# Linear attention and a GELU MLP in one kernel: batch 0 by single head pairs, first weights in two loads, h of chunk 0 over all eight banks, and the casts at its end shared anew

## The chip, the cores and the metric

The kernel runs on one core of one Trainium2 chip. The metric is the device time of one execution in microseconds (us). Engines are named as in the profile: PE is TensorE (PEld its weight loads), DVE is VectorE, ACT is ScalarE, POOL is GpSimd, SP is SyncE, which here only issues DMAs. Each engine works through a queue of its own in program order; semaphores make one wait for another.

## The reference

```
q, k, v: (8 batches, 8 heads, 576 positions, 64)          float32
q_s = softmax over the 64 of q;   k_s = softmax over the 576 positions of k
kv  = einsum('bhsd,bhse->bhde', k_s, v)
a   = einsum('bhsd,bhde->bhse', q_s, kv)
x   = a.transpose(0, 2, 1, 3).reshape(4608, 512)
h   = x @ w_in                 (512 x 2048)
g   = 0.5 * h * (1 + erf(h / sqrt(2)))
out = g @ w_out                (2048 x 512)               float32
```

## The kernel before

The tokens are worked through in nine chunks of 512: chunk b holds the first 512 positions of batch b, and the last chunk the remaining 64 of all eight batches. Matmuls are in bf16. Heads go in pairs: head pair hp (0 to 3) fills 128 partitions. The order of the work on every engine is written out by hand (`manual_schedule`); nothing is moved by a planner, so the order of the calls in the file is the order in each queue.

For batch 0 the steps are these.

- `load_main`, `load_pair`, `load_wi` and `load_wo` issue the loads on SP's queue: q, k and v of batch 0, then w_in in five pieces (`wi[0]` to `wi[4]`, 256, 256, 512, 512 and 512 columns), then w_out and the inputs of batch 1. A load of one piece of v is 0.29 MB. Each load waits in SP's queue for a semaphore that the eighth load before it sets.
- `exp_q` and `exp_k` (ACT) take the exponentials. `norm_q` sums q (DVE) and scales it (`q_scale`, line 295): heads 0 to 3 on POOL, heads 4 to 7 on DVE. `tp_mm` transposes q on PE, half of the head pairs at a time, and `tp_evac` copies it out of PSUM into `qT`.
- `cast_v` turns one head pair of v into bf16 (`v_aug`): pairs 0 and 1 on ACT (line 200), pairs 2 and 3 on POOL (line 202). `kv_mm` (line 237) makes kv for two head pairs, `kv_norm` scales it into `kvc` on DVE (lines 248 and 250). `x_mm` (line 380) makes x for two head pairs, `x_evac` copies a pair to `xT` on ACT (line 425) or DVE (line 423).
- `cast_wi_dm` and `cast_wi` turn w_in into bf16 (lines 1181 and 1169 on POOL, 1170 and 1173 on DVE), rows dm 0 to 3 of 128 each.

Then chunk 0 is done plainly (later chunks use sums that save matmuls). `h_phase` makes h for 16 tiles t of 128 columns, four matmuls each (dm 0 to 3, line 432). A group of tiles goes through dm in common, so each dm is asked for by all tiles of the group before the next one. Each tile has a PSUM bank; `h_gelu` (ACT, line 438) empties it into `g`. Functions given for a tile run after its gelu. Groups were 0 and 1 together, 2, 3, then 4 to 7, 8 to 11, and 12 to 15 one by one; banks came from 0, 1, 2 in turn, with others named for tiles 3, 6 and 8 to 11. Then `y_part(t, js)` (line 764) adds tile t of g @ w_out for the token groups js. It needs w_out in bf16: `cast_wo` (line 1207 on DVE, 1209 on ACT).

Between the y matmuls batch 1 is prepared: its exponentials, `norm_q`, `cast_v`, `tp_quarters` (PE, line 343) with `tp_quarters_evac` (DVE 353, ACT 355), kv, `kv_norm` and x. `mix_wo` (line 1226) forms sums of w_out that later chunks need. `y_out` copies y to SBUF (DVE 772, ACT 774) and stores it. `h_first` then begins h of chunk 1 (line 716).

`cast_v` is short, and its engine is the last argument:

```python
def cast_v(b, hp, eng=nc.vector):
    o = v_aug[b % 2][:, hp, :, 0:D]
    i = st[b]["vf"][:, hp, :].rearrange("p (n d) -> p n d", n=NS)
    if eng is nc.scalar:
        eng.copy(out=o, in_=i)
    else:
        eng.tensor_copy(out=o, in_=i)
```

Of the kernel before, what the change touches and what calls it, by code (L numbers as in the profile page):

```python
# [8 lines left out]
FP32 = mybir.dt.float32  # L9
# [7 lines left out]
def kernel(  # L17
# [43 lines left out]
    def bank(i, name="ps", shape=(128, 512)):  # L61
        return psum.tile(list(shape), FP32, tag=f"k{i}", name=name)
# [32 lines left out]
    def table(func):  # L95
        nc.scalar.activation(out=scr[:, 1:2], in_=scr[:, 0:1], func=func)  # L96
# [99 lines left out]
# [7 lines that stand above are left out]
# [23 lines left out]
    def kv_mm(b, half):  # L226


        if "kv" not in st[b]:
            kv_tiles(b)  # L230
        for n in range(NS):
            for i in range(2):
                for hh in range(2):
                    hp = 2 * half + i
                    pr = slice(hh * 64, hh * 64 + 64)
                    c = slice((hh ^ i) * 64, (hh ^ i) * 64 + 64)
                    nc.tensor.matmul(  # L237
                        st[b]["kv"][hp][c, 0:D + 1], ek[b % 2][pr, hp, n, :],
                        v_aug[b % 2][pr, hp, n, 0:D + 1], start=(n == 0), stop=(n == NS - 1),
                    )  # L240

    def kv_norm(b, half=None):

        if half is not None:
            hps = (2 * half, 2 * half + 1)
            rec = small.tile([128, 2], FP32, tag="reck")
            for i, hp in enumerate(hps):
                nc.vector.reciprocal(rec[:, i:i + 1], st[b]["kv"][hp][:, D:D + 1])
            for i, hp in enumerate(hps):
                nc.vector.tensor_tensor(  # L250
                    out=kvc[b][:, hp, :], in0=st[b]["kv"][hp][:, 0:D],
                    in1=rec[:, i:i + 1].to_broadcast([128, D]), op=ALU.mult,
                )
            return
        for i, ps in enumerate(st[b]["kvall"]):
            rec = small.tile([128, 2], FP32, tag="reck")
            nc.vector.reciprocal(rec, ps[:, :, D])
            nc.vector.tensor_tensor(
                out=kvc[b][:, 2 * i:2 * i + 2], in0=ps[:, :, 0:D],
                in1=rec.unsqueeze(2).to_broadcast([128, 2, D]), op=ALU.mult,  # L260
            )
# [67 lines left out]
    def tp_evac(b, half, eng="v"):  # L329
        o = st[b]["qT"][:, :, 2 * half:2 * half + 2, :]  # L330
        if eng == "v":
            nc.vector.tensor_copy(out=o, in_=st[b][f"tp{half}"])
        else:
            nc.scalar.copy(out=o, in_=st[b][f"tp{half}"])
# [30 lines left out]
    def x_tile(b, hp, pool, tag):  # L365
        if "xT" not in st[b]:
            st[b]["xT"] = attn_sb.tile([128, HP, M], BF16, tag="xT", name="xT", bufs=1)
        st[b][f"x{hp}"] = pool.tile([128, M], FP32, tag=tag, name="ps")

    def x_mm(b, half):  # L370

        for bb in range(B if b == B else 1):
            for r in range(2):
                for i in range(2):
                    hp = 2 * half + i
                    pr = slice(r * 64, r * 64 + 64)
                    c = slice((r ^ i) * 64, (r ^ i) * 64 + 64)
                    ps = st[b][f"x{hp}"]
                    if b < B:
                        nc.tensor.matmul(  # L380
                            ps[c, :], kvc_of(b, hp)[pr], st[b]["qT"][pr, :, hp, :],
                            start=True, stop=True,
                        )
                    else:
                        nc.tensor.matmul(
                            ps[c, bb * R:(bb + 1) * R], kvc_of(bb, hp)[pr],
                            st[b]["qT"][pr, bb // 2, hp, bb % 2 * R:(bb % 2 + 1) * R],
                            start=(bb == 0), stop=True, skip_group_check=True,
                        )
# [30 lines left out]
    def x_evac(b, hp, eng="v"):  # L420
        ps = st[b][f"x{hp}"]
        if eng == "v":
            nc.vector.tensor_copy(out=st[b]["xT"][:, hp, :], in_=ps)
        else:
            nc.scalar.copy(out=st[b]["xT"][:, hp, :], in_=ps)  # L425
# [4 lines left out]
    def h_mm(c, ps, t, dms):  # L430
        for dm in dms:
            nc.tensor.matmul(  # L432
                ps, wi_bf[:, dm, t * 128:(t + 1) * 128], st[c]["xT"][:, dm, :],
                start=(dm == 0), stop=(dm == NDM - 1),
            )
# [305 lines left out]

        inner(mm, seed, p5_copy, e_sum, r_sum, gelu)

    def h_phase(c, ins, groups={}, banks={}, t1=0):


        if t1 == 0:
            h_begin(c)
        while t1 < NDF:
            t0, t1 = t1, t1 + groups.get(t1, 1)  # L750
            ts = range(t0, t1)
            pss = []
            for t in ts:
                pss.append(banks[t]() if t in banks else psum_h.tile([128, M], FP32, tag="h", name="ps"))
            for dm in range(NDM):
                for ps, t in zip(pss, ts):
                    h_mm(c, ps, t, (dm,))
            for ps, t in zip(pss, ts):
                h_gelu(c, ps, t)
                for f in ins.get(t, []):  # L760
                    f()
# [7 lines left out]
    def y_out(c, ps, j, eng="v"):  # L769
        y_sb = yb4[:, j - j % 2:j - j % 2 + 2]  # L770
        if eng == "v":
            nc.vector.tensor_copy(out=y_sb[:, j % 2], in_=ps)
        else:
            nc.scalar.copy(out=y_sb[:, j % 2], in_=ps)
        if j % 2:
            y_store(c, j // 2, y_sb)
# [368 lines left out]
        store(1, 1, 0, both)  # L1145

    wi_cols = [256, 256, 512, 512, 512]
    wi_parts = [1, 1, 4, 2, 2]
    wi_off = [0, 256, 512, 1024, 1536]

    def load_wi(i):
# [23 lines left out]
    def cast_wi_dm(i, w, dm, eng):  # L1175

        n = wi_cols[i]
        r = n // 128
        o = wi_bf[:, dm, wi_off[i]:wi_off[i] + n].rearrange("p (c m) -> p c m", c=r)
        w = w[:, dm, 0:n].rearrange("p (m c) -> p c m", c=r)  # L1180
        eng.tensor_copy(out=o, in_=w)
# [22 lines left out]
    def cast_wo(i, w, c0=0, n=4, eng="v"):  # L1204
        o, w = wo_bf[:, 4 * i + c0:4 * i + c0 + n, :], w[:, c0:c0 + n]
        if eng == "v":
            nc.vector.tensor_copy(out=o, in_=w)
        else:
            nc.scalar.copy(out=o, in_=w)
# [55 lines left out]
    norm_q(0, 0, 2)  # L1265
    norm_q(0, 1, 2, nc.vector)
    tp_mm(0, 0)
    cast_v(0, 0, nc.scalar)
    cast_v(0, 1, nc.scalar)
    tp_evac(0, 0)  # L1270
    cast_v(0, 2, nc.gpsimd)
    cast_v(0, 3, nc.gpsimd)
    x_tile(0, 0, psum_y, "y")
    x_tile(0, 1, psum_y, "y")
    kv_mm(0, 0)
    kv_norm(0, 0)
    tp_mm(0, 1)
    tp_evac(0, 1, "s")
    x_tile(0, 2, psum_a, "a")
    kv_mm(0, 1)  # L1280
    kv_norm(0, 1)
    for dm in range(NDM):
        cast_wi_dm(0, wi[0], dm, nc.gpsimd)
    x_tile(0, 3, psum_h, "h")
    x_mm(0, 0)
    x_evac(0, 0, "s")
    x_evac(0, 1)
    x_mm(0, 1)
    x_evac(0, 2, "s")
    x_evac(0, 3)  # L1290
    cast_wi(1, wi[1], "pv")
    table(AF.Gelu)

    def ybank():
        return psum_y.tile([128, M], FP32, tag="y", name="ps")

    sums0 = quad_weights(0)
    h_phase(0, {
        0: [lambda: cast_wi(2, wi[2], "v")],
        2: [lambda: cast_wi(3, wi[3], "v")],  # L1300
        6: [lambda: cast_wi(4, wi[4], "v")],
        9: sums0[0:2] + [lambda: cast_wo(0, wo[0])],
        15: [lambda: cast_wo(1, wo[1], eng="s")],
    }, groups={0: 2, 4: 4, 8: 4}, banks={
        3: ybank, 6: ybank, 8: ybank,
        9: lambda: psum_a.tile([128, M], FP32, tag="a", name="ps"),
        10: lambda: bank(6), 11: lambda: bank(7),
    })


    exp_q(1, parts=2)
# [15 lines left out]
    norm_q(1, 0, 2)  # L1327
    norm_q(1, 1, 2, nc.vector)
    mix_wo(4, 0)
    for hp in range(3):  # L1330
        cast_v(1, hp, nc.gpsimd)

    def y_part(t, js):
        for j in js:
            y_mm(0, yps[j], j, t)
# [2 lines left out]
        y_part(t, range(J))  # L1338
    load_main(3, "q", q)
    mix_wo(1, 0)  # L1340
    cast_wo(3, wo[3], 2, 1)
    cast_wo(3, wo[3], 3, 1)
    mix_wo(3, 1, nc.gpsimd)
    y_part(12, range(J))
    y_part(13, range(J))
    tp_quarters(1, tps)
    kv_mm(1, 0)
    tp_quarters_evac(1, tps, 0, "v")
    tp_quarters_evac(1, tps, 1, "s")
    cast_v(1, 3, nc.scalar)  # L1350
    kv_norm(1, 0)
    y_part(14, range(J))
    y_part(15, (0, 1))
    y_out(0, yps[0], 0)
    x_tile(1, 0, Banks(5), "a")
    x_tile(1, 1, Banks(1), "h")
    x_mm(1, 0)
    y_part(15, (2,))
    kv_mm(1, 1)
    x_evac(1, 0, "s")  # L1360
    x_evac(1, 1)
    y_out(0, yps[1], 1, "s")
    kv_norm(1, 1)
    y_part(15, (3,))


    quad["r"] = wst.tile([128, 4, 2, HT], FP32, tag="w2", name="r")
# [236 lines left out]
```

## Time and profile before

| what | value |
|---|---|
| median of 3 runs | 252.5 us (252.5 to 252.83) |
| the profiled execution | 252.46 us, its span 250.7 us |
| granted clock of PE | full in the whole span |
| v of batch 0 lands | 9.64, 10.35, 11.05, 11.77 us |
| w_in lands: piece 0, piece 1 | 13.17, 14.52 us |
| first matmul of h, chunk 0 | 14.00 us |
| first matmul of y, chunk 0 | 27.82 us |
| v of batch 1 lands | 38.55, 39.09, 41.05, 41.75 us |
| last rows of w_out land | 39.73, 40.41 us |
| first matmul of h, chunk 1 | 43.70 us |

A line of the timeline reads: start, length (both us), engine, line of the kernel, operation, output<-inputs, partitions x elements and type, xcount of merged instructions, and in brackets the idle time of the engine before it with what ended it. The chain of waits lists the work that ended last, followed back from the end, with start and length. The span is the time from the first to the last instruction; the execution's own time is 1.8 us longer.

### The profile page before, as it was taken

The page shows a single profiled execution, that of the slowest core. Times are in us where ns is not written, and L with a number is a line of the kernel's source. Part 1 is how long each engine was busy: PE and PEld are TensorE (multiplying, and loading weights), DVE is VectorE, ACT ScalarE, POOL GpSimd, SP SyncE. Part 2 cuts the span into 40 slices and gives each one's busy share as a digit, 9 for nine tenths or more (in the row PEclk, how much of TensorE's full clock was granted, in tenths as well). Part 3 has the DMA queues.
Part 4 walks back from the last instruction along what each step waited for, and adds up shares of the span by engine and source line. Part 5 has one row for each costly group of instructions (what it writes and reads, how often), then busy time and mean ns, then how long its engine had stood idle before and what let it go on. Part 6 is the DMA issues. An engine that isn't in the chain of part 4 may idle for free.

```text
span 250.7 us, 7095 instructions
## 1 busy us (share of the span) xinstructions
PE 244.3 (97%) x2886; PEld 201.2 (80%) x2890; DVE 213.4 (85%) x406; ACT 193.6 (77%) x346; POOL 104.1 (42%) x130
## 2 busy tenths in 40 slices
PE   7899999999999999999999999999999999999994
PEld 3444445888888888889888988898889888998893
DVE  1978998879988978997999789979998989888972
ACT  4785988889997998899888988898881678168811
POOL 1530037490979285507940695069102920330000
PEclk9999999999999999999999999999999999999999
DMA  7999999995479949933990296600700250021015
GB/s 238 397 396 424 402 408 397 401 405 227 55 226 375 331 110 397 260 105 91 400 298 14 63 378 140 221 4 3 251 3 3 84 170 1 3 105 65 3 40 129
DMA packets 43169, 50.26 MB, mean 200 GB/s; under 512 B 20225, under 2 KB 30465, under 8 KB 42881
## 3 DMA queue, kind: packets, MB, share of 16 engines
q1 hardware_dynamic: 42416, 49.13, 59.4%
q10 hardware_dynamic: 720, 0.69, 1.1%
q8 instruction: 22, 0.36, 0.6%
q14 instruction: 11, 0.08, 0.1%
HBM read 36.70 MB, written 9.44 MB: 184 GB/s over the span
## 4 chain that ended last, share of the span: by engine, by line
PE 93%; DMA 4%; ACTq 0%; DVE 0%; POOL 0%; issue 0%
PE qa L538 20%; PE qb L538 10%; PE yba L941 8%; PE ps L764 6%; PE ps L432 6%; PE qc L538 5%; PE yba L1013 4%; PE yd L847 4%; PE ye L847 3%; PE ya L1386 3%; PE qa L716 3%; PE ya L893 3%; PE ya L1095 2%; PE kv L237 2%; PE ybb L941 2%; DMA f<-in_v_dram 2%
## 5 line engine op out<-in xcount | busy, mean ns | idle before, releaser
L538 PEld LDWEIGHTS <-quad_s 128*128 128x128 bf16 x448 | 43.7, 98 | 5.6 <-issue 0.2
L538 PEld LDWEIGHTS <-wi_bf 128*128 128x128 bf16 x336 | 32.7, 98 | 3.9 <-issue 0.2
L538 PE MATMUL qa<-quad_t,quad_s 128*128 128x256 bf16 x224 | 29.4, 272 | 0.0
L304 POOL TENSOR_TENSOR e<-e,recq 128x256 bf16<-128x256 bf16 x40 | 25.4, 672 | 0.8 <-ACT ek L190 0.8
L458 DVE TENSOR_TENSOR qb<-qa,r 128x512 f32<-128x512 f32 x32 | 20.7, 692 | 4.8 <-PE qa L538 1.7
L458 POOL TENSOR_TENSOR two<-s 128x512 bf16<-128x512 bf16 x10 | 11.6, 1158 | 30.9 <-DVE s L458 30.9
L562 ACT ACTIVATE g<-r 128x512 bf16<-128x512 f32 x28 | 17.3, 631 | 6.1 <-DVE r L458 6.1
L185 ACT ACTIVATE e<-f 128x512 bf16<-128x512 f32 (+1 forms) x44 | 20.7, 540 | 1.6 <-DMA f<-in_q_dram 1.6
L458 DVE TENSOR_TENSOR r<-qa,r 128x512 f32<-128x512 f32 x32 | 20.5, 681 | 1.1 <-PE qa L716 0.6
L202 POOL CAST v_aug<-f 128x576 bf16<-128x576 f32 x29 | 19.2, 702 | 3.8 <-DMA f<-in_v_dram 3.7
L562 ACT ACTIVATE g<-qc 128x512 bf16<-128x512 f32 x28 | 15.2, 594 | 7.1 <-PE qc L538 7.1
L425 ACT CAST xT<-ps 128x512 bf16<-128x512 f32 x23 | 12.2, 594 | 8.8 <-PE ps L380 5.3
L295 POOL TENSOR_TENSOR e<-e,recq 128x1024 bf16<-128x1024 bf16 (+1 forms) x3 | 7.4, 2476 | 26.3 <-DVE recq L290 26.3
L190 ACT ACTIVATE ek<-f 128x1152 bf16<-128x1152 f32 (+1 forms) x11 | 17.4, 1594 | 0.6 <-DMA f<-in_k_dram 0.6
L458 DVE TENSOR_TENSOR yb<-yb,yd 128x128 f32<-128x128 f32 (+2 forms) x35 | 11.9, 357 | 5.5 <-PE yd L847 3.4
L96 ACT ACT_TABLE_LOAD x11 | 14.1, 1283 | 2.8 <-issue 2.6
L562 ACT ACTIVATE g<-qb 128x512 bf16<-128x512 f32 x28 | 15.0, 585 | 0.9 <-PE qb L538 0.9
L538 PE MATMUL qb<-quad_t,quad_s 128*128 128x256 bf16 x112 | 15.5, 272 | 0.0
L538 PE MATMUL qa<-xT,wi_bf 128*128 128x256 bf16 x112 | 15.3, 273 | 0.0
L562 ACT ACTIVATE g<-qa 128x512 bf16<-128x512 f32 x28 | 15.3, 610 | 0.0
L941 PEld LDWEIGHTS <-g 128*128 128x128 bf16 x144 | 13.7, 98 | 1.4
L538 PE MATMUL qc<-xT,wi_bf 128*128 128x256 bf16 x112 | 14.5, 272 | 0.0
(191 smaller groups left out, 622.6 us busy)
## 6 DMA issues: line engine op xcount, KB each, us to landing
out_dram<-yb SPq DMA_DIRECT2D x16, 512.0 KB, 3.6
f<-in_k_dram SPq DMA_DIRECT2D x6, 1152.0 KB, 7.6
f<-in_v_dram SPq DMA_DIRECT2D x6, 1152.0 KB, 10.6
f<-in_q_dram SPq DMA_DIRECT2D x6, 1024.0 KB, 11.4
w<-in_moe_w_in_dram SPq DMA_DIRECT2D x6, 512.0 KB, 8.6
f<-in_v_dram SPq DMA_DIRECT2D x8, 288.0 KB, 6.4
f<-in_q_dram SPq DMA_DIRECT2D x4, 512.0 KB, 8.8
w<-in_moe_w_out_dram SPq DMA_DIRECT2D x2, 1024.0 KB, 11.7
```

Of the source, the lines that this page charges most:

```text
L96: nc.scalar.activation(out=scr[:, 1:2], in_=scr[:, 0:1], func=func)
L185: nc.scalar.activation(out=dst[:, i, js], in_=src[:, u, js], func=AF.Exp)
L190: nc.scalar.activation(out=ek[b % 2][:, i:i + n], in_=st[b]["kf"][:, i:i + n].rearrange("p x (n d) -> p x n d", n=NS), func=AF.Exp,)
L202: eng.tensor_copy(out=o, in_=i)
L304: nc.gpsimd.tensor_tensor(out=e, in0=e, op=ALU.mult, in1=st[b]["recq"][:, j, i:i + 4].unsqueeze(2).to_broadcast([128, 4, D]),)
L432: nc.tensor.matmul(ps, wi_bf[:, dm, t * 128:(t + 1) * 128], st[c]["xT"][:, dm, :], start=(dm == 0), stop=(dm == NDM - 1),)
L458: eng.tensor_tensor(out=out, in0=in0, in1=in1, op=op)
L538: nc.tensor.matmul(held[kind, q][:, u], w, mov[m][:, k], start=(m in (1, 5) and u == 0 and k == 0), stop=(k == 1), skip_group_check=True,)
L562: nc.scalar.activation(out=g[:, t:t + 2, half], in_=held[kind, q], func=AF.Gelu)
L764: nc.tensor.matmul(ps, st[c]["g"][:, t, j * 128:(j + 1) * 128], wo_bf[:, t, :], start=(t == 0), stop=(t == NDF - 1),)
L847: nc.tensor.matmul(getattr(self, at)[:, r * 128:(r + 1) * 128], lhs, rhs, start=first, stop=(i == 3), skip_group_check=True,)
L941: nc.tensor.matmul(ps[:, j * HN:(j + 1) * HN], act[m][:, k, j * 128:(j + 1) * 128], wgt[m][:, k, :], start=(first and k == 0 and j == 0), ...
```

## The change

The four casts of v of batch 0 all go to POOL. Kv, its scaling and x of batch 0 go by single head pairs (`kv_pair`, `x_pair`, and `kv_norm` with a list of pairs) in another order; the transposed halves of q change engines; x of pair 3 is made inside h's first group, after dm 0, through the new argument `mid`. Pieces 0 and 1 of w_in are loaded in two halves each, piece 3 in four parts. H of chunk 0 goes in groups of 2, 2, 4, 4 and 4 tiles with a fixed turn of all eight banks. `cast_wo(0)` goes in two halves between sums. At the end of the chunk the casts of v of batch 1 are on POOL, DVE, POOL, POOL instead of POOL, POOL, POOL, ACT, `cast_wo(3, ..)` is moved around, and the two `y_out` change engines and places, with one matmul group of y moved ahead.

```diff
+    def kv_pair(b, hp):
+        if "kv" not in st[b]:
+            kv_tiles(b)
+        for n in range(NS):
+            for hh in range(2):
+                pr = slice(hh * 64, hh * 64 + 64)
+                c = slice((hh ^ hp % 2) * 64, (hh ^ hp % 2) * 64 + 64)
+                nc.tensor.matmul(
+                    st[b]["kv"][hp][c, 0:D + 1], ek[b % 2][pr, hp, n, :],
+                    v_aug[b % 2][pr, hp, n, 0:D + 1], start=(n == 0), stop=(n == NS - 1),
+                )
+
+    def x_pair(b, hp):
+        for r in range(2):
+            pr = slice(r * 64, r * 64 + 64)
+            c = slice((r ^ hp % 2) * 64, (r ^ hp % 2) * 64 + 64)
+            nc.tensor.matmul(
+                st[b][f"x{hp}"][c, :], kvc_of(b, hp)[pr], st[b]["qT"][pr, :, hp, :],
+                start=True, stop=True,
+            )
...
-    def kv_norm(b, half=None):
-        if half is not None:
-            hps = (2 * half, 2 * half + 1)
+    def kv_norm(b, half=None, hps=None):
+        if half is not None or hps:
+            hps = hps or (2 * half, 2 * half + 1)
...
-    def h_phase(c, ins, groups={}, banks={}, t1=0):
+    def h_phase(c, ins, groups={}, banks={}, t1=0, mid={}):
...
             for dm in range(NDM):
                 for ps, t in zip(pss, ts):
                     h_mm(c, ps, t, (dm,))
+                if (t0, dm) in mid:
+                    mid[t0, dm]()
...
-    wi_parts = [1, 1, 4, 2, 2]
+    wi_parts = [2, 2, 4, 4, 2]
...
     tp_mm(0, 0)
-    cast_v(0, 0, nc.scalar)
-    cast_v(0, 1, nc.scalar)
-    tp_evac(0, 0)
-    cast_v(0, 2, nc.gpsimd)
-    cast_v(0, 3, nc.gpsimd)
+    for hp in range(HP):
+        cast_v(0, hp, nc.gpsimd)
+    tp_evac(0, 0, "s")
     x_tile(0, 0, psum_y, "y")
     x_tile(0, 1, psum_y, "y")
-    kv_mm(0, 0)
-    kv_norm(0, 0)
+    kv_pair(0, 0)
+    kv_norm(0, hps=(0,))
     tp_mm(0, 1)
-    tp_evac(0, 1, "s")
+    tp_evac(0, 1)
+    x_pair(0, 0)
+    x_evac(0, 0, "s")
+    kv_pair(0, 1)
+    kv_pair(0, 2)
+    kv_norm(0, hps=(1, 2))
     x_tile(0, 2, psum_a, "a")
-    kv_mm(0, 1)
-    kv_norm(0, 1)
+    kv_pair(0, 3)
+    kv_norm(0, hps=(3,))
     for dm in range(NDM):
         cast_wi_dm(0, wi[0], dm, nc.gpsimd)
+    x_pair(0, 1)
+    x_evac(0, 1, "s")
+    x_pair(0, 2)
+    x_evac(0, 2)
     x_tile(0, 3, psum_h, "h")
-    x_mm(0, 0)
-    x_evac(0, 0, "s")
-    x_evac(0, 1)
-    x_mm(0, 1)
-    x_evac(0, 2, "s")
-    x_evac(0, 3)
     cast_wi(1, wi[1], "pv")
-    table(AF.Gelu)
+
+    def x_last():
+        x_pair(0, 3)
+        x_evac(0, 3, "s")
+        table(AF.Gelu)
...
-        9: sums0[0:2] + [lambda: cast_wo(0, wo[0])],
+        9: [lambda: cast_wo(0, wo[0], 0, 2), sums0[0], lambda: cast_wo(0, wo[0], 2, 2), sums0[1]],
         15: [lambda: cast_wo(1, wo[1], eng="s")],
-    }, groups={0: 2, 4: 4, 8: 4}, banks={
-        3: ybank, 6: ybank, 8: ybank,
-        9: lambda: psum_a.tile([128, M], FP32, tag="a", name="ps"),
-        10: lambda: bank(6), 11: lambda: bank(7),
-    })
+    }, groups={0: 2, 2: 2, 4: 4, 8: 4, 12: 4},
+        banks={t: lambda i=i: bank(i) for t, i in enumerate([1, 2, 0, 3, 4, 5, 6, 7] * 2)},
+        mid={(0, 0): x_last})
...
-    for hp in range(3):
-        cast_v(1, hp, nc.gpsimd)
+    cast_v(1, 0, nc.gpsimd)
...
     mix_wo(1, 0)
+    cast_v(1, 1)
     cast_wo(3, wo[3], 2, 1)
-    cast_wo(3, wo[3], 3, 1)
-    mix_wo(3, 1, nc.gpsimd)
+    for hp in (2, 3):
+        cast_v(1, hp, nc.gpsimd)
     y_part(12, range(J))
     y_part(13, range(J))
     tp_quarters(1, tps)
     kv_mm(1, 0)
     tp_quarters_evac(1, tps, 0, "v")
     tp_quarters_evac(1, tps, 1, "s")
-    cast_v(1, 3, nc.scalar)
+    cast_wo(3, wo[3], 3, 1)
+    mix_wo(3, 1, nc.gpsimd)
     kv_norm(1, 0)
     y_part(14, range(J))
-    y_part(15, (0, 1))
-    y_out(0, yps[0], 0)
+    y_part(15, (0, 1, 2))
+    y_out(0, yps[0], 0, "s")
+    y_out(0, yps[1], 1)
     x_tile(1, 0, Banks(5), "a")
     x_tile(1, 1, Banks(1), "h")
     x_mm(1, 0)
-    y_part(15, (2,))
-    kv_mm(1, 1)
     x_evac(1, 0, "s")
     x_evac(1, 1)
-    y_out(0, yps[1], 1, "s")
+    y_part(15, (3,))
+    kv_mm(1, 1)
     kv_norm(1, 1)
-    y_part(15, (3,))
```

More of the change, by code (lines that the diff above doesn't have):

```diff
@@ L1267 @@
     tp_mm(0, 0)
-    cast_v(0, 0, nc.scalar)
-    cast_v(0, 1, nc.scalar)
-    tp_evac(0, 0)
-    cast_v(0, 2, nc.gpsimd)
-    cast_v(0, 3, nc.gpsimd)
+    for hp in range(HP):
+        cast_v(0, hp, nc.gpsimd)
+    tp_evac(0, 0, "s")
     x_tile(0, 0, psum_y, "y")
     x_tile(0, 1, psum_y, "y")
-    kv_mm(0, 0)
-    kv_norm(0, 0)
+    kv_pair(0, 0)
+    kv_norm(0, hps=(0,))
     tp_mm(0, 1)
-    tp_evac(0, 1, "s")
+    tp_evac(0, 1)
[4 more added lines that the diff above has]
+    kv_norm(0, hps=(1, 2))
     x_tile(0, 2, psum_a, "a")
-    kv_mm(0, 1)
-    kv_norm(0, 1)
+    kv_pair(0, 3)
+    kv_norm(0, hps=(3,))
     for dm in range(NDM):
         cast_wi_dm(0, wi[0], dm, nc.gpsimd)
+    x_pair(0, 1)
+    x_evac(0, 1, "s")
+    x_pair(0, 2)
+    x_evac(0, 2)
     x_tile(0, 3, psum_h, "h")
-    x_mm(0, 0)
-    x_evac(0, 0, "s")
-    x_evac(0, 1)
-    x_mm(0, 1)
-    x_evac(0, 2, "s")
-    x_evac(0, 3)
     cast_wi(1, wi[1], "pv")
-    table(AF.Gelu)
-    def ybank():
-        return psum_y.tile([128, M], FP32, tag="y", name="ps")
+    def x_last():
+        x_pair(0, 3)
+        x_evac(0, 3, "s")
+        table(AF.Gelu)
     sums0 = quad_weights(0)
```

## The prediction

> **What bounds the kernel now.** I read the page first, then the chain of waits, then the timeline of the first 16 us and of 35 to 44 us, the two stretches that the diff edits. Page:
>
> ```profile
> span 250.7 us, 7095 instructions
> PE 244.3 (97%) x2886; PEld 201.2 (80%) x2890; DVE 213.4 (85%) x406; ACT 193.6 (77%) x346; POOL 104.1 (42%) x130
> PE 93%; DMA 4%; ACTq 0%; DVE 0%; POOL 0%; issue 0%
> ```
>
> TensorE is the bound. From the first matmul of h at 14.00 us on no idle gap of PE is longer than 0.07 us. So the time can move in two ways only: h begins at another moment, or a new wait opens behind it. The chain of waits in front of h:
>
> ```profile
> 6.59 5.18 DMA f<-in_v_dram
> 11.82 0.68 POOL v_aug L202
> 12.54 0.52 PE kv L237 x34
> 13.53 0.54 PE ps L380 x4
> ```
>
> The last piece of v lands at 11.77, its cast ends at 12.49, then kv, its scaling, x, h. The timeline shows what stands beside it (start, length, engine, line):
>
> ```profile
> 7.92 1.90 POOL L295 TENSOR_TENSOR e<-e,recq 128x1024 bf16<-128x1024 bf16 x1 [6.62 <-DVE recq L290]
> ...
> 9.24 1.67 DVE L295 TENSOR_TENSOR e<-e,recq 128x1024 bf16<-128x1024 bf16 x1
> ...
> 9.97 1.23 ACT L200 CAST v_aug<-f 128x576 bf16<-128x576 f32 x2
> ...
> 11.10 1.39 POOL L202 CAST v_aug<-f 128x576 bf16<-128x576 f32 x2 [1.27 <-DMA f<-in_v_dram]
> ...
> 35.02 1.90 POOL L295 TENSOR_TENSOR e<-e,recq 128x1024 bf16<-128x1024 bf16 x1 [19.73 <-DVE recq L290]
> ...
> 36.29 1.72 DVE L295 TENSOR_TENSOR e<-e,recq 128x1024 bf16<-128x1024 bf16 x1
> ...
> 38.53 0.68 DVE L1226 TENSOR_TENSOR wo_bf<-wo_bf 128x1024 bf16<-128x1024 bf16 x1
> 38.61 1.73 POOL L202 CAST v_aug<-f 128x576 bf16<-128x576 f32 x2 [1.69 <-DMA f<-in_v_dram]
> ...
> 39.75 1.20 DVE L1207 CAST wo_bf<-w 128x512 bf16<-128x512 f32 x2 [0.55 <-DMA w<-in_moe_w_out_dram]
> ```
>
> Read the pairs. DVE's scaling of q (L295) ends 1.09 us after POOL's both times (10.91 against 9.82, 38.01 against 36.92), though it began 0.58 and 0.63 us before that end: it stood still while POOL worked. The other way round, two POOL casts take 1.73 us beside a DVE product of two SBUF tiles, instead of 1.28 (0.61 from start to start, 0.67 for the last); the first ends 0.52 us after the DVE instruction. The DVE cast at 39.75 waits for POOL too (0.87 us; the next one 0.41). DVE evacuations from PSUM and reductions are not slowed.
>
> **The v casts.** Casts 0 and 1 leave ACT (0.66 us each, beside other work) for POOL, in front of 2 and 3. POOL is free at 9.82, and that is when the DVE scaling, waiting since 9.24, takes its turn until 10.91. No row shows a POOL cast beside this very DVE instruction, so its end lies between 10.43 (no wait) and 11.43 (10.91 + 0.52). I take 11.43, because the same instruction was itself held up by POOL, and a DVE product at 38.53 held up just such a cast. At 0.61 us each the casts then end at 11.43, 12.04, 12.65 and 13.26; the last was 12.49. The Trainium skill ("SBUF — State Buffer", section "Who interferes with whom") says that a DVE instruction with two SBUF inputs contends with a GpSimd one that reads SBUF, the loser blocking fully. The trace agrees for the DVE side (1.67 and 1.72 us); POOL's side of this pair no run here shows yet.
>
> **Kv and x by pairs.** Kv of pair 0 runs from 11.48, the second transposes to 12.36, their DVE evacuation (0.68) to 13.09. Kv of pair 2 runs from 12.70 to 13.04. Two reciprocals and two products (0.5 us by the rows of L248 and L250) give kvc 1 and 2 at 13.47 and 13.60, the x pairs start at 13.52 and 13.66, and the first matmul of h at 13.66 + 0.22 + 0.10 = 13.98. The 0.10 is what PE loses between 64-row and 128-row matmuls (transposes issued last at 12.05 and 0.055 apart, next kv weights 12.20; y to x at 42.31, 42.40). The second matmul of h is at 14.20. Then the inserted x pair 3 (its kvc is ready at 14.15) takes 0.22 and two changes of 0.10, so dm 1 starts at 14.83. The other xT tiles are there in time (14.53, 14.80, 15.52 for 14.83, 15.26, 15.69). Sixteen matmuls end at 14.83 + 14 x 0.2157 = 17.85; before, 14.00 + 16 x 0.2157 = 17.45. **Front: +0.40 us.** Without the POOL wait h begins at 13.21 and the same sum gives 17.08, that is -0.37.
>
> **First weights in two loads, wi 3 in four.** Four more SP issues of 0.3 to 0.5 us. SP is 6 us ahead of the landings, and a load goes out when the eighth before it lands (issue 10.37, landing 10.35), so eight of 0.26 MB, some 5 us of traffic, stay outstanding: no queue runs dry. Bounds: 0 to +0.1. I take 0, as 0.26 MB loads of wi 2 land 0.62 to 0.76 us apart and 0.5 MB ones 1.25 to 1.40. The first half of wi 0 would land near 12.5, but POOL comes to it at 13.2 (13.22 before): no gain either; if POOL does not wait, it helps it begin at 12.5. The Trainium skill (the same page, section "The DMA setup-cost knee") speaks against small loads: each pays a roughly fixed 2 us. By it the second half of wi 0 would come some 2 us later, as an estimate; the spacing of the landings does not agree.
>
> **Eight banks, groups of 2, 2, 4, 4, 4.** The same 64 matmuls, back to back before and after: 0 gained. The last four gelus now come together: 0.60 us each, 0.49 apart, the first 0.42 us after t 12's last matmul starts, so `cast_wo(1)` on ACT ends 4.28 us after that start, and y's t 4 asks for it after 20 x 0.2157 = 4.31. 0, with bounds 0 and +0.1. ACT is then 1.2 us later than before (31.6 against 30.4); exp of q 1 waited 0.36 and 0.16 us for its loads, which swallows part, and the scaling of q 1 on DVE ends at 38.6 instead of 38.0, ahead of its transposes at 40.4. `cast_wo(0)` in halves: nothing, it is done at 26.5 and y begins near 28.2.
>
> **End of chunk 0.** With +0.40 kv of pairs 0 and 1 starts at 40.93. Its casts: POOL's first at 39.7, DVE's (after `mix_wo(1, 0)`, which waits for that POOL cast) near 40.75: in time by 0.1. Behind it DVE's queue holds `cast_wo(3, 2)`, the evacuation of the transposes (from 41.20), `cast_wo(3, 3)` (41.80), `kv_norm(1, 0)`, `y_out` 1, the evacuation of x 1. `cast_wo(3, 3)` meets POOL's casts of v 2 (41.10 to 41.77) and v 3 (from 41.80, landing 41.75): if it goes between them, `kv_norm` ends at 42.65 and x starts at 42.97, when PE comes to it. Then `y_out` 1 stands ahead of x 1's evacuation: y 15 ends at 42.81, copy to 43.47, x 1 to 44.15, so the second matmul of the next h waits until 44.20, where PE was free at 44.06. **+0.15.** The y matmul moved from behind kv to before it costs nothing. Later mixes on POOL start 0.7 us later but wait for `quad_t` at 47.4 anyway.
>
> **Sum.** +0.40 + 0.15 = +0.55. The profiled execution took 252.46 us (span 250.7), the median is 252.5: 253.0. About 0.2%, 0.5 us, is what a measurement of this kernel can tell from no change.
>
> **Rivals.**
> - A, POOL does not wait for the DVE scaling (not slower). For: no row shows this pair. Against: the rows above. H starts at 13.21, -0.37; the end of the chunk gives back 0.15 because the evacuations are tied to landings: 252.3. It decides at the end of the first cast: below 10.6. If `cast_wo(3, 3)` then falls behind POOL's cast at 41.10 (margin 0.07), +0.42 instead: also within 0.2%.
> - B, `cast_wo(3, 3)` loses to POOL's cast of v 3 at 41.80. DVE then waits until about 42.3, `kv_norm` ends near 43.2, x starts at 43.5: +1.1, 253.6. The two issue times are equal to 0.05 us; only which is first decides.
> - C, the front costs under 0.1 (x overlaps more, a change of shape is cheaper), yet `cast_wo(3, 3)` waits for POOL's cast at 41.10, which lifts any front cost between -0.25 and +0.25 to +0.42: 252.9.
> - D, small loads pay their fixed price: +2, 254.5.
> - E, something that these rows do not show saves over 0.5. PE has no idle time behind 14 us to give back, so little speaks for it.
>
> **How the numbers follow.** Forecast 0.46 (its own range +0.40 to +0.75, about two thirds of it over 0.5), A 0.15, B 0.22, C 0.09, D 0.02, E 0.06. Slower: 0.32 + 0.22 + 0.02 = 0.56. Same: 0.14 + 0.15 + 0.09 = 0.38. Faster: 0.06. The range from 252.2 (A) to 253.8 (B and 0.2 for the bounds of loads and gelus) leaves out D and E and a little of A.
>
> **What would show it.** Right: POOL's first v cast of about 1.6 us ending at 11.4, the last at 13.3; h's first two matmuls near 14.0, a hole of 0.6 before the third; y from 28.2; PE idle 0.1 us near 44.1. Wrong: a first cast of 0.67 us, h from 13.2, or a y that starts before 27.8 with no new gap of PE behind it.

## The result, and the profile after

| | before | after |
|---|---|---|
| median | 252.5 us (252.32 to 252.83, 6 runs) | 254.22 us (253.57 to 254.49, 6 runs) |
| ratio | 1 | 1.0063, interval 1.0049 to 1.0076 |
| profiled execution, span | 252.46, 250.7 us | 254.25, 252.4 us |
| scaling of q on POOL begins | 7.92 us | 8.13 us |
| y of chunk 0 begins | 27.82 us | 28.56 us |
| h of chunk 1 begins | 43.70 us | 45.14 us |
| PE ends | 246.96 us | 248.71 us |

The kernel is 0.63% slower, 1.7 us; forecast were 0.5 us, with an upper end of 253.8. The page of after:

```profile
span 252.4 us, 7099 instructions
PE 244.9 (97%) x2886; PEld 201.4 (80%) x2890; DVE 214.5 (85%) x407; ACT 191.9 (76%) x344; POOL 106.0 (42%) x132
PE 87%; DVE 4%; ACT 3%; POOL 2%; DMA 2%; issue 0%; POOLq 0%
```

PE is as busy as before to 0.6 us, but the chain that ended last now runs over DVE, ACT and POOL for 9% of the span instead of about none. The chain of waits says where it leaves PE (start, length):

```profile
8.13 1.90 POOL e L317
10.03 3.44 POOL v_aug L202 x4
...
15.23 10.90 PE ps L454 x50
...
28.11 2.06 ACT g L460 x4
...
37.45 1.73 DVE e L317
...
40.85 0.66 DVE v_aug L202
...
42.45 0.83 DVE wo_bf L1231
43.31 0.81 PE ps L788 x3
```

Two places: in front of h all four casts of v now stand on POOL, and at the end of the chunk the cast of v 1 and the cast of the last rows of w_out stand on DVE. Between them the chain runs over ACT's last gelus, which end at 30.18 us (before 28.62), and over DVE's scaling of q 1, which ends at 39.18 us (before 38.01), so DVE comes late to its cast of v 1. The timeline of the first place (start, length, engine, line):

```profile
9.44 1.67 DVE L317 TENSOR_TENSOR e<-e,recq 128x1024 bf16<-128x1024 bf16 x1
9.97 1.66 POOL L202 CAST v_aug<-f 128x576 bf16<-128x576 f32 x1
...
14.30 0.39 PE L454 MATMUL ps<-xT,wi_bf 128*128 128x512 bf16 x1
14.83 0.40 PE L259 MATMUL ps<-qT,kvc 64*64 64x512 bf16 x2
15.17 0.39 PE L454 MATMUL ps<-xT,wi_bf 128*128 128x512 bf16 x1
```

POOL's first cast takes 1.66 us where the next three take 0.66 each: it ends 0.52 us after DVE's scaling of q, at 11.63. One of the two engines stood still while the other worked; below this is called the lock. Then x of pair 3 opens a hole in h before dm 1. The second place:

```profile
40.77 0.74 DVE L202 CAST v_aug<-f 128x576 bf16<-128x576 f32 x1
41.27 0.78 PE L237 MATMUL kv<-v_aug,ek 64*64 64x65 bf16 x36
41.56 1.42 POOL L202 CAST v_aug<-f 128x576 bf16<-128x576 f32 x2 [1.86 <-DMA f<-in_v_dram]
42.37 0.90 DVE L1231 CAST wo_bf<-w 128x512 bf16<-128x512 f32 x1
43.31 0.38 PE L788 MATMUL ps<-wo_bf,g 128*128 128x512 bf16 x1 [0.30 <-DVE wo_bf L1231]
```

Before, kv of batch 1 ran through:

```profile
40.53 0.54 PE L237 MATMUL kv<-v_aug,ek 64*64 64x65 bf16 x36
```

Kv takes 0.78 us where it took 0.54, as its second half waits for DVE's cast of v 1. `cast_wo(3,3)` takes 0.90 us where the one before it took 0.41: it stood beside POOL's second cast, and y of tile 15 waited for it. The 0.30 us in brackets count from the end that the profile gives the last matmul; from start to start the gap is 0.68 us where y matmuls otherwise follow each other every 0.22, so 0.46 us were lost.

Where PE lost the 1.79 us by which the two profiled executions differ, read from the starts of its instructions: 0.21 up to the scaling of q on POOL (q of batch 0 landed at 5.17 instead of 4.96); 0.53 from there to the first y; 0.24 at kv of batch 1; 0.46 from y 15 to h of chunk 1; 0.09 in small pieces to 106 us; 0.16 at 107.5; 0.06 after that. Those are 1.75, and 0.04 lie behind PE's last matmul.

The 0.21 are not apart from the change. In the profiles of the eight kernels with the old front (before and seven of the experiments below) the first y begins 16.05 to 16.17 us after the last piece of v lands, even where the scaling of q begins as late as 8.40 us. In after and its three variants with all casts on POOL it begins 20.43 us after the scaling begins, and 16.79 to 16.95 us after v lands. The old front hangs on the landing of v, the new one on that of q.

### The profile page after: what moved, and what is told of

Read it like the earlier page. It is cut to its first block, busy times and chain, and to the rows that moved or that the text cites. A ratio compares the mean times of both kernels' runs of the same rounds, so it can differ in the third digit from the quotient of the medians.

```text
span 252.4 us, 7099 instructions
## 1 busy us (share of the span) xinstructions
PE 244.9 (97%) x2886; PEld 201.4 (80%) x2890; DVE 214.5 (85%) x407; ACT 191.9 (76%) x344; POOL 106.0 (42%) x132
## 4 chain that ended last, share of the span: by engine, by line
PE 87%; DVE 4%; ACT 3%; POOL 2%; DMA 2%; issue 0%; POOLq 0%
PE qa L560 20%; PE qb L560 10%; PE yba L965 8%; PE ps L454 5%; PE qc L560 5%; PE yba L1037 4%; PE yd L871 4%; PE qa L738 3%; PE ya L1410 3%; PE ye L871 3%; PE ya L917 3%; PE ya L1119 2%; PE ybb L965 2%; PE yf L871 2%; PE kv L237 2%; DMA f<-in_q_dram 2%
## 5 line engine op out<-in xcount | busy, mean ns | idle before, releaser
L202 POOL CAST v_aug<-f 128x576 bf16<-128x576 f32 x31 | 21.2, 722 | 2.6 <-DMA f<-in_v_dram 2.6
L447 ACT CAST xT<-ps 128x512 bf16<-128x512 f32 x24 | 12.8, 594 | 10.6 <-PE ps L402 4.7
L788 PE MATMUL ps<-wo_bf,g 128*128 128x512 bf16 x62 | 14.4, 379 | 0.4 <-DVE wo_bf L1231 0.3
```

The lines of the kernel that those rows point to most:

```text
L788: nc.tensor.matmul(ps, st[c]["g"][:, t, j * 128:(j + 1) * 128], wo_bf[:, t, :], start=(t == 0), stop=(t == NDF - 1),)
```

## The experiments

Each run has the kernel before beside it on the same chip; its median was 252.47 in the first four runs, 252.67 in the next four, then 252.51 and 252.44. A kernel's excess below is against that.

**Each part alone.** `front_only` has the diff from the casts of v to `x_last`, `loads_only` the line `wi_parts`, `groups_only` the groups, banks and halves of `cast_wo(0)`, `end_only` the hunks behind `mix_wo(4, 0)`.

> The kernel before with only the front of the change: all four v casts on POOL, kv, scaling and x by single head pairs, x of pair 3 inside the first group of h; loads, groups, banks and the end of chunk 0 as before. Theory 1 (the parts add up, each by its own wait): POOL's first cast waits for DVE's scaling of q (about 1.66 us instead of 0.66), h loses about 0.5 us by its sixteenth matmul, and since PE has no idle time behind it the end comes 0.4 to 0.6 us later. Theory 2 (the split loads set the loss, since every landing from w_in on is about 0.45 us later in the changed kernel): under 0.2 us.

> The kernel before with only w_in's pieces 0, 1 and 3 loaded in more parts (14 loads instead of 10). Both theories: the landings behind w_in come 0.4 to 0.5 us later (0.1 to 0.16 for each added load). Theory 1: kv of batch 1 then waits for its v, +0.2 to +0.3 us at the end. Theory 2: +0.5 to +1.0 us. If the later landings in the changed kernel are chance: 0 and no shift.

> The kernel before with only h of chunk 0 in groups of 2, 2, 4, 4, 4 over eight banks and the first cast of w_out in halves. Theory 1: the same matmuls back to back, ACT about 0.8 us later at the end of h, swallowed by its waits for loads: 0 to +0.2 us. Theory 2: 0.

> The kernel before with only the end of chunk 0 in the new order (v casts of batch 1 on POOL, DVE, POOL, POOL, cast_wo(3, ..) and the two y_out moved). Theory 1: the last cast of w_out stands behind the evacuation of the transposes and waits for POOL's cast of v 2 that begins near 41.1, y of tile 15 or x waits for it: +0.4 us. Theory 2: with the landings as before it is in time: within 0.15 us.

| kernel | median | ratio, interval | h of chunk 1 |
|---|---|---|---|
| front_only | 253.78 | 1.0051, 1.0038 to 1.0065 | 44.39 |
| loads_only | 252.36 | 0.9997, 0.9988 to 1.0005 | 43.77 |
| groups_only | 252.55 | 1.0006, 0.9997 to 1.0015 | 43.68 |
| end_only | 253.5 | 1.0039, 1.0027 to 1.0052 | 44.23 |

Loads and groups alone cost nothing, and the 0.2 to 0.3 us that theory 1 expected of the loads did not come. Front and end cost 1.3 and 1.0 us, and that is more than PE lost in them by the start of h of chunk 1: 0.69 and 0.53 us. So each had some 0.5 us more, far from its own lines, which neither theory had. In `front_only` DVE stood idle 0.30 us at 106.6 with no releaser in the profile, and in both the last store of ACT began late.

**The lock in front.** `v_pool` is the kernel before with the casts on POOL and nothing else; `front_act` is the new front without that.

```diff
 # v_pool, from before           # front_act, from front_only
-cast_v(0, 0, nc.scalar)         -cast_v(0, hp, nc.gpsimd)
-cast_v(0, 1, nc.scalar)         +cast_v(0, hp, nc.scalar if hp < 2 else nc.gpsimd)
+cast_v(0, 0, nc.gpsimd)
+cast_v(0, 1, nc.gpsimd)
```

> The kernel before with one edit: the casts of v 0 and 1 of batch 0 go to POOL, ahead of 2 and 3; kv and x stay by halves. Two tiny activations more on ACT (454 instructions as before). Theory 'lock': POOL's first cast takes about 1.65 us beside DVE's scaling of q, the last cast ends 0.8 us later than before (13.3 for 12.5) and, as kv by halves waits for it, h begins 0.8 later: 253.3. Theory 'pairs' (the order costs, not the casts): POOL has all four casts done by 12.5, as the last v lands at 11.7: 252.5.

> The front of the changed kernel alone, but the casts of v of pairs 0 and 1 stay on ACT (POOL casts 2 and 3), and one memset of one column more on DVE (533 instructions as before). Theory 'lock' (the front costs what POOL's cast loses to DVE's scaling of q): the casts end as before, h begins near 13.3 and its 16 matmuls end near 17.1, 0.3 earlier than before; the time is 252.1 to 252.6, as loads land when they did and may give part back at the end of chunk 0. Theory 'pairs' (single pairs and the x inside h cost it): the front stays 0.3 to 0.5 later than before, 252.8 to 253.0.

`v_pool` took 253.47 us (1.0041, 1.0029 to 1.0054). Its timeline:

```profile
9.81 3.49 POOL L202 CAST v_aug<-f 128x576 bf16<-128x576 f32 x4
...
14.81 1.04 PE L432 MATMUL ps<-xT,wi_bf 128*128 128x512 bf16 x4
```

The first cast takes 1.66 us again, the last ends at 13.30, and from the scaling of q to the first y it is 0.77 us longer than before (20.67 for 19.90), as 'lock' said. In all seven kernels with four casts on POOL the first takes 1.66 us and ends 0.52 to 0.53 us after DVE's scaling; no kernel moved DVE's instruction instead. `front_act` took 252.69 us (1.0002, 0.9993 to 1.0011):

```profile
9.82 1.23 ACT L200 CAST v_aug<-f 128x576 bf16<-128x576 f32 x2
10.93 1.39 POOL L202 CAST v_aug<-f 128x576 bf16<-128x576 f32 x2 [0.93 <-DMA f<-in_v_dram]
13.62 0.60 PE L454 MATMUL ps<-xT,wi_bf 128*128 128x512 bf16 x2
```

No long cast, h 0.4 us earlier than before, and 19.82 us from the scaling to y, 0.08 less than before. That is no gain: the eight profiles with the old front lie between 19.57 and 19.97 us, and counted from the landing of the last v the first y comes after 16.32 us, 0.15 to 0.27 more than theirs. X of pair 3 inside h takes back more than the earlier start of h gives, and x of pair 0 waits for ACT, whose copy of `qT` stands here behind its casts of v:

```profile
12.01 0.40 PE L259 MATMUL ps<-qT,kvc 64*64 64x512 bf16 x2 [0.25 <-ACT qT L356]
```

'Lock' was right on the cause and wrong on what is left without it (0.3 us earlier was expected); 'pairs' was right that the rest costs something. What single pairs are worth with ACT free as well was not run. At the end of the chunk the last rows of w_out landed at 41.30 here (before 40.41), their cast and the evacuation behind it came late on DVE, and h of chunk 1 began at 44.17.

**The end of the chunk.** Both kernels are `end_only` with one edit.

```diff
 # end_wo3
 cast_wo(3, wo[3], 2, 1)
+cast_wo(3, wo[3], 3, 1)
...
 tp_quarters_evac(1, tps, 1, "s")
-cast_wo(3, wo[3], 3, 1)
 # end_v1
 cast_v(1, 0, nc.gpsimd)
+cast_v(1, 1, nc.gpsimd)
...
 mix_wo(1, 0)
-cast_v(1, 1)
```

> The end of the chunk as changed, but cast_wo(3,3) right behind cast_wo(3,2) on DVE, ahead of the evacuation of the transposes, so ahead of POOL's casts of v 2 and 3; one tiny activation more on ACT (454 instructions as before). Theory 'the cast of the last rows of w_out loses to POOL': the wait of 0.24 us of PE in y 15 goes, the wait for the DVE cast of v 1 stays: h of chunk 1 begins 0.25 to 0.3 later than before instead of 0.53, 252.7 to 252.8. Theory 'the cast of v 1 on DVE pushes all behind it': y 15's wait shrinks but the evacuation of q and x come 0.4 later, no gain, 253.0 to 253.1. In both the late last stores are gone if they hang on ACT's instruction count.

> The end of the chunk as changed, but the cast of v 1 of batch 1 on POOL behind v 0 again (not on DVE behind the sums of w_out); one tiny instruction more on ACT and one on DVE (454 and 533 as before). cast_wo(3,3) stays where the change put it. DVE is then some 0.6 us earlier in its queue and comes to the evacuation of the transposes at 41.0, to cast_wo(3,3) at 41.5: beside POOL's cast of v 2, or just ahead of it. Theory 'place beside POOL's casts': it still loses to POOL, y 15 waits, h of chunk 1 0.2 to 0.5 later than before, 252.8 to 253.0. Theory 'the late cast of v 1 pushes all behind it': both waits go, 252.5 to 252.6.

`end_wo3` took 252.53 us (0.9995, 0.9986 to 1.0004), `end_v1` 252.9 (1.0016, 1.0008 to 1.0025). End_wo3's timeline, then end_v1's:

```profile
40.54 0.75 DVE L1231 CAST wo_bf<-w 128x512 bf16<-128x512 f32 x2
41.08 1.68 PE L788 MATMUL ps<-wo_bf,g 128*128 128x512 bf16 x7
```

```profile
41.47 0.82 DVE L1231 CAST wo_bf<-w 128x512 bf16<-128x512 f32 x1
42.35 0.81 PE L788 MATMUL ps<-wo_bf,g 128*128 128x512 bf16 x3 [0.22 <-DVE wo_bf L1231]
```

Ahead of POOL's casts, which begin at 41.37, both rows are cast in 0.75 us together, y runs through, and h of chunk 1 begins 0.08 us later than before. The wait for v 1, which was expected to stay, is nearly gone too: DVE's cast ended 0.03 us after kv began. With v 1 back on POOL the wait for v 1 is gone, but the cast of the last rows still stands beside POOL's (0.82 us), y 15 still waits and h begins 0.47 later. The place of `cast_wo(3,3)` is the costly edit; the late cast of v 1 is not what pushes it there. End_v1 lost another 0.33 us at 98 us, at a place that this edit does not touch: there PE waited for DVE's `kvc`, behind a DVE sum of two SBUF tiles that took 0.92 us beside POOL's products instead of 0.58.

**The place in the queue.** DVE's idle time and the late stores stood only in kernels whose ACT or DVE had one or two instructions less than before. So these kernels only add tiny instructions at the start, where both engines are idle, or take one away.

```diff
 table(AF.Exp)
+for _ in range(n):                          # ACT: n more
+    table(AF.Exp)
+nc.vector.memset(scr[:, 2:3], 0.0)          # DVE: one more
 # before_short
-nc.vector.memset(scr, 0.0)
+nc.gpsimd.memset(scr, 0.0)
-... moe_w_in[0:128:8, 0:2], moe_w_out[0:512:32, 0:2])):
+... moe_w_in[0:128:8, 0:2])):
```

> The changed kernel with three tiny instructions more at the start, where ACT and DVE are idle: two more of the activations of line 96 (ACT) and one memset of one column (DVE). ACT then has as many instructions as the kernel before (454) and DVE too (533). Theory 'position in the instruction stream': the idle 0.3 us of DVE before qb at 107.4 and the late last stores hang only on which instruction of ACT and DVE stands where: both go, 0.5 to 0.65 us faster than the changed kernel, 253.6 to 253.7, with the PE timeline up to 106 us the same as in the changed kernel. Theory 'real waits' (the hole and the tail are waits for data that the change makes late): nothing changes, 254.2.

> The kernel before with one instruction less on ACT (the tiny load of w_out on ACT's queue, which only touches the tensor) and one less on DVE (the memset of the 3 columns goes to POOL). Nothing else changes. Theory 'position in the instruction stream': the hole of 0.3 us before qb at 106 us opens (+0.2 on PE) and the last stores end 0.3 to 0.45 later: 253.0 to 253.15. Theory 'real waits': 252.5.

> The changed kernel with one tiny memset more on DVE and nothing else (DVE 533 instructions, ACT still 452). Theory 'every 64th instruction of a queue starts some 0.3 us late': the idle time of DVE before qb at 107.4 goes (0.15 to 0.2 us of PE), the late last stores stay: 253.9 to 254.1. Theory 'real waits': 254.2.

> The front of the changed kernel alone, with one tiny instruction more on ACT and one on DVE, where both are idle (454 and 533 instructions, as before). Theory 'every 64th instruction of a queue starts some 0.3 us late': DVE's idle time before qb at 106.6 goes, and the last store ends 0.4 sooner after PE's end; 0.5 to 0.65 us less than without the two (253.78): 253.1 to 253.3. What stays is POOL's locked cast. Theory 'real waits': 253.8.

> The end of the chunk as changed, with one tiny activation more on ACT (454 instructions, as before). Theory 'every 64th instruction starts some 0.3 us late': the last store ends 0.4 us sooner after PE's end, 0.3 to 0.45 less than without it (253.5): 253.05 to 253.2, and what stays is cast_wo(3,3) behind POOL's casts. Theory 'real waits': 253.5.

| kernel | instructions of ACT, DVE | median | ratio, interval | DVE idle before `qb` | profiled execution less PE's end |
|---|---|---|---|---|---|
| before | 454, 533 | 252.5 | | 0 | 5.50 |
| after | 452, 532 | 254.22 | 1.0063, 1.0049 to 1.0076 | 0.32 | 5.54 |
| after_dve1 | 452, 533 | 253.86 | 1.0048, 1.0036 to 1.006 | 0 | 5.47 |
| after_pad | 454, 533 | 253.47 | 1.0031, 1.0019 to 1.0042 | 0 | 5.22 |
| front_only | 453, 532 | 253.78 | 1.0051, 1.0038 to 1.0065 | 0.30 | 5.95 |
| front_pad | 454, 533 | 253.09 | 1.0025, 1.0015 to 1.0034 | 0 | 5.49 |
| end_only | 453, 533 | 253.5 | 1.0039, 1.0027 to 1.0052 | 0 | 5.98 |
| end_pad | 454, 533 | 252.66 | 1.0009, 0.9998 to 1.002 | 0 | 5.48 |
| before_short | 453, 532 | 253.46 | 1.0038, 1.0026 to 1.0051 | 0.31 | 5.74 |

Front_only's timeline of DVE, then front_pad's:

```profile
105.38 0.96 DVE L480 TENSOR_TENSOR s<-g 128x1024 bf16<-128x1024 bf16 x1
106.64 1.30 DVE L480 TENSOR_TENSOR qb<-qa,r 128x512 f32<-128x512 f32 x2 [0.30 <-issue]
```

```profile
105.32 0.95 DVE L480 TENSOR_TENSOR s<-g 128x1024 bf16<-128x1024 bf16 x1
106.22 1.30 DVE L480 TENSOR_TENSOR qb<-qa,r 128x512 f32<-128x512 f32 x2
```

The same two instructions, idle between them only in the first. Counted through its queue, `qb` is DVE's 192nd instruction in every kernel with 532 of them, and the 193rd in every one with 533. At the end it is ACT's 448th: in all these kernels it begins 0.32 to 0.34 us after the one before it ended. With 454 instructions that is a store with slack behind it, with 453 the wait directly ahead of the last store, with 452 the last store itself. End_only, then end_pad, stores on ACT's queue beside DVE's last product:

```profile
247.57 0.29 DVE L480 TENSOR_TENSOR yb<-yb,yd 128x128 f32<-128x128 f32 x1
248.09 0.47 ACTq L1110 DMA_DIRECT2D out_dram<-yb  x1
```

```profile
247.39 1.18 ACTq L1110 DMA_DIRECT2D out_dram<-yb  x2
247.62 0.29 DVE L480 TENSOR_TENSOR yb<-yb,yd 128x128 f32<-128x128 f32 x1
```

In end_pad the second of the two stores begins at 247.98, 0.08 us behind the product's end; in end_only it begins 0.23 behind. PE ends at 247.53 and 247.58 in these two profiles and y 15 waits in both, yet their executions took 253.51 and 253.06 us. In front the two tiny instructions took the excess from 1.31 to 0.65 us. 'Real waits' fell in both. Before_short, the kernel before with two instructions less, is 0.79 us slower than it, though not all of that is DVE and ACT: its v landed 0.15 us later and its front began 0.16 later; POOL, which got the memset, stood idle 1.17 us at 92.8 instead of 0.85, and PE lost another 0.30 at 98, behind the same DVE sum as in `end_v1` (0.92 us again). That idle time on POOL is as long in the other two kernels with 173 instructions there (1.17 and 1.21 us) and 0.80 to 0.86 us in all with another number, but it is not the loss itself: one of the two, `after_fix`, lost nothing at 98.

What was not expected is in after_pad and after_dve1: they differ from after in tiny instructions alone, yet h of chunk 1 begins at 44.80 and 44.63 instead of 45.14. After_dve1's timeline beside after's above:

```profile
41.62 1.63 POOL L202 CAST v_aug<-f 128x576 bf16<-128x576 f32 x2 [1.97 <-DMA f<-in_v_dram]
41.92 1.68 PE L788 MATMUL ps<-wo_bf,g 128*128 128x512 bf16 x7
42.32 0.41 DVE L1231 CAST wo_bf<-w 128x512 bf16<-128x512 f32 x1
```

Here DVE's cast went between POOL's two (0.41 us) and POOL's second one was held up instead. In after_pad it took 0.70. POOL's casts begin when v 2 lands (41.51, 41.57 and 41.92 us in after, after_dve1 and after_pad) and DVE's when its queue comes to it, so the order looks like a race that is decided anew in each execution. One execution of each kernel was traced, so this is argued: end_pad's runs lie from 252.38 to 252.75 (seven) and from 253.02 to 253.58 (four, the traced one with the wait among them), which fits it, and puts end_pad's median below the 253.05 that was expected. After_pad's median is not all of it a matter of the queue.

**Together.** `after_wo3` is after_pad with the edit of end_wo3. `after_fix` is the changed kernel with that edit, the casts of v 0 and 1 on ACT and one memset more on DVE.

> The changed kernel with cast_wo(3,3) right behind cast_wo(3,2), and the three tiny instructions (ACT 454, DVE 533). The locked cast of v stays. Theory 'three causes': y 15 no longer waits whichever way the race between DVE and POOL goes, the front's 0.4 to 0.55 us and some 0.15 of the late cast of v 1 stay: h of chunk 1 begins 0.6 to 0.8 later than before, 253.1 to 253.3, with a smaller spread than the changed kernel has. Theory 'the evacuation behind it becomes late': 253.5 or more.

> The changed kernel with three things undone: the casts of v 0 and 1 of batch 0 on ACT again, cast_wo(3,3) right behind cast_wo(3,2), and one tiny memset more on DVE (ACT then has 454 and DVE 533 instructions, as before). Theory 'three causes' (POOL's cast locked by DVE's scaling, the cast of the last rows of w_out behind POOL's casts, the place of an instruction in its queue): nearly all of the 1.6 us goes, h of chunk 1 begins at 43.8 to 44.2, 252.6 to 252.9. Theory 'the rest of the change costs too' (single pairs, x inside h, new order of y_out): at least 0.5 us stays, 253.1 or more.

After_wo3 took 253.21 us (1.0027, 1.0016 to 1.0038; 252.93 to 253.34) and its h of chunk 1 begins at 44.63, 0.93 later than before, of which 0.69 is the front (0.16 of them with a later q) and 0.24 the late cast of v 1. No wait at y 15, and a spread of 0.41 us where the changed kernel has 0.92. After_fix took 252.98 us (1.0021, 1.0012 to 1.003; 44.12): most of the 1.7 us is gone, 0.47 stays, a little over what 'three causes' expected. Its profile puts 0.17 into the front (single pairs, x inside h, and x of pair 0 waiting 0.45 us for ACT's copy of `qT`) and 0.24 into DVE's cast of v 1, which was not undone; this execution was the shortest of its eleven (252.66), so not all of the median's 0.47 is placed. So both theories are right in part. No version was faster than the kernel before.

## Why the prediction was wrong

- **The lock** (right, to 0.01 us). Counted from the start of POOL's scaling of q, the first cast would end 3.51 us after it; it ended 3.50 after it, and the others followed 0.61 apart. The rule of the Trainium skill ("SBUF — State Buffer", section "Who interferes with whom") that was cited for it is borne out on POOL's side too: POOL's first cast of batch 0 took 1.66 us in the seven kernels where it met DVE's scaling, and 0.66 to 0.69 in the others.
- **Front** (+0.40 forecast; +0.53 measured from the scaling of q to y, the same in after and its three variants that keep the locked cast, and 0.74 with the later q). `kvc` of pairs 1 and 2 was ready 0.1 us later than reckoned, so x and the first matmul of h were, and the hole before dm 1 was 0.02 larger. The sum also set both fronts on one profile's clock, though the new one hangs on q and the old one on v: in after q landed 0.21 us later and v 0.16 earlier, and the forecast had no term for that. Rival A fell with the first cast. Its price, -0.37 for the front without the wait, was not tested: front_act and after_fix, whose casts ended as early as before, had their first y 0.1 to 0.3 us later, counted from the landing of v, but there x of pair 0 waited for ACT, which A leaves free.
- **Loads and groups** (0 forecast, 0 measured). The two halves of piece 0 landed 0.67 us apart in after (12.69 and 13.36) and cost nothing. So the fixed 2 us of the section "The DMA setup-cost knee" of the same page of the Trainium skill, which the forecast's estimate laid on each load, do not add up over loads that are queued behind each other; rival D fell.
- **End of the chunk** (+0.15 forecast, +0.70 in the profile). This is the step that failed. The forecast let `cast_wo(3,3)` go between POOL's casts and gave rival B, that it loses, a third of what it gave both. Of the six profiles of kernels that put it there it lost in four (in after to the cast of v 3, as in B; in end_only, end_pad and end_v1 to that of v 2, as in C), took 0.70 us in one (after_pad) and won in one (after_dve1). The price of B, 0.7 above the front, equals the 0.70 measured only by luck: the lost turn cost 0.46, at y 15 itself and not at x behind `kv_norm` as B had it, and the other 0.24 come from the cast of v 1 on DVE: "in time by 0.1" in the forecast, it ended 0.25 us after kv began. The forecast let ACT's waits for loads swallow half of ACT's delay, so that the scaling of q 1 would end at 38.6; it ended at 39.18. The forecast's own term of 0.15, a late copy of y 1 ahead of the evacuation of x 1, did not appear: h of chunk 1 runs through.
- **What the forecast had no term for.** DVE's idle 0.3 us at 107.4 (0.16 us of PE) comes from counting one instruction less. In the kernels with one part it was 0.5 to 0.7 us with the late last store; in the changed kernel with ACT at 452 the store is late (0.69 us after PE's end instead of 0.40) but the execution ended only 0.04 later by the profile. The split loads gave the rest back, which the forecast did not have either. At its end SP waits for the stores' semaphores in a fixed order, some 0.06 us for each; where w_in comes in ten loads the last store's is the first of five (SP is through 0.33 us after its landing in before), where it comes in fourteen the last store has the last one (0.08 us in loads_only). The profiled executions with 454 instructions on ACT ended 5.48 to 5.52 us after PE in all seven kernels with ten loads, and 5.22 to 5.25 in all four with fourteen. Why the later store of after landed sooner than that of end_only (2.88 and 3.10 us after PE's end) stays open.
- **Sum.** 0.53, 0.24, 0.46 and 0.16 are 1.39 us. The profile has 0.21 more from q, 0.15 in pieces too small to follow and 0.04 behind PE's end. After_pad and after_wo3, where the queue and at last the race are taken out, came to 0.80 and 0.77 us: that would lie inside the range, and still above its centre.

## What to carry to other kernels

When a cast is moved to GpSimd or between its casts, write down which VectorE instruction with SBUF operands runs at that moment; here the lock made one cast 1.0 us longer and cost 0.46 us in the other place, and in the change and two variants that differ in tiny instructions alone the same cast took 0.90, 0.70 and 0.41 us. Put the one whose result TensorE needs next ahead of the contention, in the program's order. Ask also which landing each chain hangs on: moving work behind another engine's can exchange one landing for another, as v for q here. And before a small difference is explained by a wait, count the instructions of each engine in both kernels: one more or less moved variants of this kernel by 0.5 to 0.7 us.

## What the hardware showed that was not expected

- An instruction at a fixed place of its engine's queue began some 0.3 us late: DVE's 192nd (0.30 to 0.32 us where nothing covered it), ACT's 448th (0.32 to 0.34 us in all kernels). Both are odd multiples of 64; DVE's 448th shows no such gap, and the runs do not tell the rule. The DMA table of the profile has a kind "instruction" whose transfers on one queue are 8 KB each; one of them comes 0.55 to 0.92 us after PE's end in the kernels with 454 or 455 and 1.4 to 1.7 after it in those with 452 or 453 instructions on ACT, so loading the instructions is a likely cause, which was argued and not tried. The Trainium skill ("Runtime: NRT & Kernel Launch", section "Instruction fetch mechanics") says that instructions are loaded in blocks and that crossing a boundary is mostly hidden. If these gaps are such crossings, they are hidden here only where the instruction has slack.
- The lock between DVE and POOL shows far from the change too: in v_pool a DVE sum of two SBUF tiles at 97.1 took 0.93 us beside POOL's products instead of 0.58, and PE lost 0.32 us there. In end_v1 and before_short it took 0.92, and PE lost 0.33 and 0.30; in the other fourteen profiles it took 0.43 to 0.59 and PE lost nothing.
